# Four score tiles in five adjacent PSUM banks, and the FFN gate in SBUF

## The chip, the cores and the metric

The kernel runs on one core of one Trainium2 chip. The metric is the device time of one execution in microseconds (us); shown is the median of several runs. Beside it stands one execution taken by the hardware profiler, whose span goes from the first to the last instruction.

## The reference

Sparse attention is followed by a feed-forward network (FFN); all sizes are fixed.

```
q, k, v: 8 batches x 8 heads x 576 positions x 64      (float32)
scores = q @ k.T / 8;  keep scores >= max(row) - tau;  attn = softmax of those kept, sum + 1e-9
x = attn @ v, laid out as 4608 tokens x 512
h = x @ w_in (512 x 2048);  g = h if h >= 1, 0 if h <= -1, else (h + 1)^2 / 4
out = g @ w_out (2048 x 512)                            (float32; the weights arrive as float64)
```

## The kernel before

Each factor of a product is split into two float16 parts, high and low, and the product is made of three passes (high x high, high x low, low x high).

**Attention.** The 576 query rows of a head are cut into tiles of 128 rows; a tile's scores are 128 x 576 float32 in PSUM. A *visit* on TensorE (PE) computes two tiles at once, one of each head of a pair: the head dimension of 64 fills half of PE's rows, so the matmuls of the two heads run side by side. Each tile uses two PSUM banks, 288 columns in each (`s_ps`, two buffers); both buffers are taken by every visit. The rows that are left over are visited as a *tail*, 64 rows of two heads in one tile. The tile then goes through this chain (`add_tile`):

- DVE scales it in place and takes its minimum (L1039), and adds the threshold (L1043);
- ACT takes the exponential into SBUF, tile `e` (L1046);
- DVE masks it and sums the row (L1060), and takes the reciprocal (L1070);
- then one of three ways. Way "P", 283 of the 288 tiles: POOL scales `e` (L1078), ACT makes the high part `hl` (L1083), POOL the low part (L1086). Way "S", 3 tiles: DVE masks in PSUM (L1094), ACT makes the high part from there (L1102), DVE the low part (L1105). Way "T", 2 tiles: the transpose is done on PE;
- SP starts a DMA that transposes `hl` into `eT` (L1108), and PE multiplies by the values (L1184); ACT and DVE split that into `x` (L1192, L1196).

**FFN.** For 256 tokens at a time (128 in places), step by step of 256 or 512 hidden units: PE makes `ph` in PSUM (first product, L461), ACT takes relu and square into `asq` in SBUF (L1259, L1262), DVE forms the gate in place in `ph` (L1266), ACT makes the high part from `ph` (L1271, two instructions a step), DVE the low part from `ph` and the high part (L1276, two a step), both into `ga` and `gb` (some of whose buffers are free parts of the weight tiles `WI` and `WO`), and PE adds the second product into `acc` (L461). The PSUM ring `ph` has three banks; they also serve the attention-value product and small sums. PSUM is full: four banks for scores, three for `ph`, one for `acc`.

**Other work of two SBUF inputs on DVE.** The low part of some q and k tiles (L605, where `QHOW` has "D") and of the values (L661) is made by DVE from two tiles in SBUF.

**Order.** Every operation is an entry of a plan, with a cost and its buffers. The table `ORDER` gives the sequence in which a planner walks the entries; it computes a start for each from the costs, and the instructions are emitted in order of these starts, so each engine's queue is fixed by the program. SP's queue holds all DMA issues; an instruction in it that waits holds up those behind it. Small matmuls on `ones` (L1337) fill idle stretches of PE in the first 200 us.

Of the kernel before, what the change touches and what calls it, by code (L numbers as in the profile page):

```python
# [12 lines left out]
U32 = mybir.dt.uint32  # L13
AF = mybir.ActivationFunctionType
# [1379 lines left out]
```

## Time and profile before

| | us |
|---|---|
| median of 3 runs (1110.39 to 1111.41) | 1110.39 |
| the profiled execution | 1114.32 |
| its span | 1112.5 |
| PE busy in the span | 1080.0 (97%) |
| DVE busy | 898.6 (81%) |
| ACT busy | 871.3 (78%) |
| POOL busy | 789.5 (71%) |

Times in the rows are in us unless marked ns. Rows of groups give line, engine, operation, output and inputs, shape and count, then busy time, mean ns of one, and the idle time in front of them with what ended it. Rows of a timeline give start, duration and instruction. PEld is the loading of weights into PE, SPq the queue of SP. TensorE was granted 0.991 of its clock over the span.

### The profile page before, as it was taken

The numbers are of one execution on the slowest core, as the hardware profiler recorded it, in microseconds if no ns is written. First come the engines' busy times: TensorE is split into PE (matmuls) and PEld (weight loads), VectorE is DVE, ScalarE is ACT, GpSimd is POOL, SyncE is SP. The second block draws the span as 40 slices with busy tenths as digits, with TensorE's granted clock in tenths as the row PEclk, the third lists the DMA queues.
The fourth block names the chain that finished last, engine by engine and source line by source line (L and its number), as shares of the span: only waits on it lengthen the run. The fifth ranks groups of instructions, "written<-read, shape, count | busy, mean of one in ns | idle before, by whom it ended". The sixth has DMA issues, their size and how long they took to land.

```text
span 1112.5 us, 37005 instructions
## 1 busy us (share of the span) xinstructions
PE 1080.0 (97%) x14703; PEld 793.3 (71%) x14703; DVE 898.6 (81%) x2668; ACT 871.3 (78%) x1675; POOL 789.5 (71%) x921
## 2 busy tenths in 40 slices
PE   8689999999999999999999999999999999999998
PEld 7457657777777667776777677677777677777774
DVE  5899989998888887898788888788788898887222
ACT  6889769798797887887787888778788886776433
POOL 5889998786877987797768886666667987565000
PEclk9889999999999999999999999999999999999999
DMA  9887888688796997679867866759776686656000
GB/s 343 331 215 125 142 169 160 119 154 145 116 165 127 167 157 142 118 143 174 141 119 137 156 127 131 136 106 177 128 144 104 128 126 113 123 104 119 11 21 20
DMA packets 418046, 155.25 MB, mean 140 GB/s; under 512 B 396880, under 2 KB 396880, under 8 KB 417872
## 3 DMA queue, kind: packets, MB, share of 16 engines
q1 hardware_dynamic: 417872, 152.88, 70.9%
q8 instruction: 115, 1.88, 0.7%
q14 instruction: 59, 0.48, 0.1%
HBM read 45.09 MB, written 9.44 MB: 49 GB/s over the span
## 4 chain that ended last, share of the span: by engine, by line
PE 77%; DVE 8%; ACT 4%; DMA 4%; POOL 3%; issue 2%; SPq 0%; DVEq 0%; ACTq 0%; POOLq 0%
PE ph L461 30%; PE acc L461 28%; PE s L986 9%; PE ph L1184 8%; DMA eT<-hl 3%; DVE s L1039 2%; DVE e L1060 1%; POOL hl L1086 1%; ACT hl L1083 1%; PE ph L1337 1%; ACT e L1046 1%; POOL e L1078 1%; DMA raw<-in_k_dram 0%; DMA WO<-in_moe_w_in_dram 0%; DVE sm L1043 0%
## 5 line engine op out<-in xcount | busy, mean ns | idle before, releaser
L1086 POOL TENSOR_TENSOR hl<-e,hl 128x576 f16<-128x576 f32 x283 | 363.7, 1291 | 119.2 <-ACT hl L1083 112.4
L461 PEld LDWEIGHTS <-WI 128*64 128x64 f16 (+1 forms) x7458 | 408.0, 108 | 52.1 <-issue 15.1
L461 PE MATMUL ph<-x,WI 128*64 128x256 f16 (+1 forms) x6912 | 400.5, 264 | 0.3 <-DVE WI L1276 0.2
L1078 POOL TENSOR_SCALAR e<-e,sm 128x576 f32<-128x576 f32 x283 | 218.7, 776 | 77.8 <-DVE sm L1070 60.3
L1039 DVE TENSOR_SCALAR_CACHE_REDUCE s<-s,pc 128x576 f32<-128x576 f32 x288 | 230.9, 819 | 53.1 <-PE s L986 52.1
L1060 DVE SCALAR_TENSOR_TENSOR e<-s,sm,e 128x578 f32<-128x578 f32 x283 | 228.5, 814 | 29.3 <-ACT e L1046 21.5
L1046 ACT ACTIVATE e<-s,sm 128x576 f32<-128x576 f32 x288 | 209.7, 740 | 48.4 <-DVE s L1039 41.1
L1083 ACT ACTIVATE hl<-e 128x576 f16<-128x576 f32 x283 | 190.9, 681 | 55.5 <-POOL e L1078 38.8
L461 PE MATMUL acc<-WO,ga 128*64 128x512 f16 (+1 forms) x1596 | 203.3, 380 | 0.0
L1259 ACT ACTIVATE asq<-ph,fcs 128x512 f32<-128x512 f32 (+1 forms) x160 | 115.9, 735 | 44.7 <-PE ph L461 43.1
L1266 DVE SCALAR_TENSOR_TENSOR ph<-ph,fcs,asq 128x512 f32<-128x512 f32 (+1 forms) x160 | 111.3, 699 | 48.5 <-ACT asq L1262 47.7
L461 PEld LDWEIGHTS <-ga 128*64 128x64 f16 (+1 forms) x1596 | 92.5, 109 | 80.7 <-issue 9.0
L986 PE MATMUL s<-kk,qq 64*128 64x288 f16 (+1 forms) x1920 | 142.4, 286 | 7.3 <-DVE e L1060 4.3
L1184 PE MATMUL ph<-eT,vst 128*64 128x320 f16 (+2 forms) x1928 | 122.5, 279 | 7.1 <-DMA eT<-hl 3.8
L986 PEld LDWEIGHTS <-qq 64*128 64x128 f16 (+1 forms) x1920 | 80.9, 97 | 64.1 <-issue 45.7
L1184 PEld LDWEIGHTS <-vst 128*64 128x64 f16 x1928 | 100.6, 110 | 27.0 <-issue 12.4
L1262 ACT ACTIVATE asq<-asq 128x512 f32<-128x512 f32 x144 | 90.6, 630 | 3.1
L1276 DVE SCALAR_TENSOR_TENSOR ga<-ph,fcs,ga 128x256 f16<-128x256 f32 (+1 forms) x160 | 70.6, 449 | 23.8 <-ACT WO L1271 9.3
L1271 ACT ACTIVATE ga<-ph,fcs 128x256 f16<-128x256 f32 (+1 forms) x160 | 70.3, 450 | 24.0 <-DVE ph L1266 21.8
L461 PE MATMUL acc<-WO,gb 128*64 128x512 f16 (+1 forms) x576 | 73.9, 380 | 0.0
L461 PE MATMUL acc<-WO,WI 128*64 128x512 f16 (+1 forms) x546 | 69.9, 380 | 0.0
L461 PE MATMUL acc<-WO 128*64 128x512 f16 (+1 forms) x510 | 64.5, 380 | 0.0
(184 smaller groups left out, 1122.3 us busy)
## 6 DMA issues: line engine op xcount, KB each, us to landing
raw<-in_v_dram SPq DMA_DIRECT2D x32, 288.0 KB, 3.3
raw<-in_q_dram SPq DMA_DIRECT2D x32, 288.0 KB, 3.5
raw<-in_k_dram SPq DMA_DIRECT2D x32, 288.0 KB, 3.5
WO<-in_moe_w_in_dram SPq DMA_DIRECT2D x16, 512.0 KB, 7.7
out_dram<-ob SPq DMA_DIRECT2D x32, 256.0 KB, 2.5
x<-in_moe_w_out_dram SPq DMA_DIRECT2D x10, 512.0 KB, 5.6
eT<-hl SPq DMA_TRANSPOSE x286, 3.5
WO<-in_moe_w_out_dram SPq DMA_DIRECT2D x4, 512.0 KB, 5.0
```

What stands on the lines that cost most here:

```text
L461: T.matmul(out[x], lhsT[:, x], rhs, **flags)
L986: T.matmul(ap(sb, s_ps)[r, f, :SH], ap(qb, qq)[h, ql, c : c + r.stop - r.start], ap(kb, kk)[h, kl, f * SH : (f + 1) * SH], start=ql == kl ...
L1039: V.tensor_scalar(sv(), sv(), c[:, 24 + v : 25 + v], None, ALU.mult, ALU.min, accum_out=t[:, 0:1])
L1046: A.activation(ev(), sv(), AF.Exp, bias=ap(m, sm)[:, 0:1], scale=-1.0)
L1060: V.scalar_tensor_tensor(ev(SH + 1), sv(SH + 1), t[:, 2:3], ev(SH + 1), ALU.is_le, ALU.mult, accum_out=t[:, 3:4])
L1078: G.tensor_scalar(ev(), ev(), ap(m, sm)[:, 5:6], ESC, ALU.mult, ALU.mult)
L1083: A.activation(part2(0), ev(), AF.Copy)
L1086: G.tensor_tensor(part2(w), ev(), part2(0), ALU.subtract)
L1184: T.matmul(o[hd * D : (hd + 1) * D, :n], vt[:, k, hd * D : (hd + 1) * D], t[:, kb, (hd ^ p % 2) * n : ((hd ^ p % 2) + 1) * n], start=m == ...
L1259: A.activation(tv()[:, :, c], hv()[:, :, c], AF.Relu, bias=fcs[:, b, 2, q : q + 1], scale=fcs[:, b, 3, q : q + 1])
L1262: A.activation(ap(tb, asq), ap(tb, asq), AF.Square)
L1266: V.scalar_tensor_tensor(hv()[:, :, c], hv()[:, :, c], fcs[:, b, 0, q : q + 1], tv()[:, :, c], ALU.max, ALU.min)
```

## The change

From the second half of batch 1 on, a visit scores four tiles: two of each head, in one PSUM tile `s_all` of five adjacent banks. The tiles lie 578 columns apart and cross bank borders, so each is written in two pieces; the pieces of the two heads that run side by side lie in different banks. One bank holds pieces of both heads, the last of the first pair of tiles and one of the second pair; a no-op on SP (called the gate below, L1025 of the new kernel), which waits for PE's last write of the first and is waited for by PE ahead of the second, keeps these apart. Tails use the same tile. Of the 144 visits, 52 pairs of full ones become 52 visits of four; the fifth bank is taken from the ring `ph`, which keeps two.

In the FFN the gate is written into `asq` in SBUF instead of back into `ph` (L1377), and the high and low parts are made from there (L1382, L1387); the ring `asq` grows from two to four buffers. Way "S" is replaced by a way "V", taken by 32 tiles: DVE masks as in "P" and takes one more small operation, ACT makes the high part from `e` in SBUF, DVE the low part from `e` and `hl` (L1205). 255 tiles stay on "P" and one on "T". In the weights' preparation and for q and k some units change engines (`CONV`, `SIGN`, `QHOW`), and `ORDER` is a new table.

```diff
-CONV = {"i": "GGMGPGGPPPGPMPQP", "o": "PAPADPPAPDPDDADD"}
+CONV = {"i": "GGPGPGGPPPGPMPPQ", "o": "PAMADPPADGPPDAMD"}
-QHOW = "DDPDPPDPPPDPPPPPPPPPPPPPPDDPPPPP"
+QHOW = "DDPDPPDPPPDDPDPPPPPPPPPPPDDPPPPP"
+FOURS = 16
 ORDER = [
-    0, 54, 58, 59, 56, 57, 60, 623, 633, 638, 1, 4, 628, 5, 2, 55, 658, 61, 648, 653, 625, 643, 62, 63, 64, 900, 80, 624, 626, 627, 634, 75, 635, 636,
...
-TILE = {0: "T", 1: "T", 71: "S", 214: "S", 287: "S"}
+TILE = {0: "T", 1: "V", 3: "V", 21: "V", 25: "V", 33: "V", 38: "V", 53: "V", 74: "V", 78: "V",
...
-    s_ps = [pp.tile([P, 2, 512], F32, name=f"s{i}") for i in range(2)]
+    s_all = pp.tile([P, 5 * 512], F32, name="s")
+    s_ps = [s_all[:, i : i + 1024].rearrange("p (f n) -> p f n", f=2) for i in (0, 1024)]
-    ph = [pp.tile([P, 512], F32, name=f"ph{i}") for i in range(3)]
+    ph = [pp.tile([P, 512], F32, name=f"ph{i}") for i in range(2)] + [s_all[:, 2048:]]
-    asq = ring("asq", 2, [FW], F32)
+    asq = ring("asq", 4, [FW], F32)
...
+    def where(k):
+        x = sixth + k * (S + 2)
+        return x, -(-x // 512) * 512 - x
+    def add_four(js, slots):
+        toks = [plan.buf("s"), plan.buf("s")]
...
+            for a, z in ((0, 2),) if tail else ((0, 2), (1, 3)):
+                (fa, ca), (fz, cz) = pieces(at[a], a), pieces(at[z], z)
+                early, late = ((fz, 0, cz), (fa, 0, ca)), ((fz, cz, S), (fa, ca, S))
+                lows = ((0, 0), (0, 1), (1, 0))
+                walk = [(l, early + late) for l in lows] if not a else [(l, early) for l in lows] + [(l, late) for l in lows]
+                for (ql, kl), parts_ in walk:
+                    for fs, u, w in parts_:
+                        for f in fs:
+                            n = f(ql, kl, u, w)
+                        if fs is fz and not a and not u and ql and not tail:
+                            gate = Y.nop()
+                            tc.add_manual_dep(gate.ins, n.ins.name, DependencyInfo(DependencyClass.Sync, DependencyReason.DATA), reason="two row groups in a bank")
+                        if fs is fa and a and u and ql == kl == 0:
+                            tc.add_manual_dep(n.ins, gate.ins.name, DependencyInfo(DependencyClass.Sync, DependencyReason.DATA), reason="two row groups in a bank")
...
+        if not tail:
+            plan.op("SP", 0.75, lambda: None, behind=o)
...
+        def lo_v():
+            V.scalar_tensor_tensor(part2(w), ev(), ap(m, sm)[:, 5:6], part2(0), ALU.mult, ALU.subtract)
...
             def gate(hv=hv, tv=tv, g=g, q=q):
-                    V.scalar_tensor_tensor(hv()[:, :, c], hv()[:, :, c], fcs[:, b, 0, q : q + 1], tv()[:, :, c], ALU.max, ALU.min)
+                    V.scalar_tensor_tensor(tv()[:, :, c], hv()[:, :, c], fcs[:, b, 0, q : q + 1], tv()[:, :, c], ALU.max, ALU.min)
-                        A.activation(gv(h, 0)[:, :, c], hv()[:, 2 * h : 2 * h + 2, c], AF.Copy, scale=fcs[:, b, 1, q : q + 1])
+                        A.activation(gv(h, 0)[:, :, c], tv()[:, 2 * h : 2 * h + 2, c], AF.Copy, scale=fcs[:, b, 1, q : q + 1])
-                        V.scalar_tensor_tensor(gv(h, 1)[:, :, c], hv()[:, 2 * h : 2 * h + 2, c], fcs[:, b, 1, q : q + 1], gv(h, 0)[:, :, c], ALU.mult, ALU.subtract)
+                        V.scalar_tensor_tensor(gv(h, 1)[:, :, c], tv()[:, 2 * h : 2 * h + 2, c], fcs[:, b, 1, q : q + 1], gv(h, 0)[:, :, c], ALU.mult, ALU.subtract)
```

Three places in the order of the instructions follow. On PE, a visit before, in a batch's middle: `s` are the scores, `kk` and `qq` the split keys and queries; two tiles, 12 matmuls of 288 columns, then the attention-value product.

```order
L461 MATMUL acc<-WO,ga_107 64x512
L986 LDWEIGHTS qq_83
L986 MATMUL s_62<-kk_79,qq_83 128x288
L986 MATMUL s_61<-kk_79,qq_83 128x288
L1184 LDWEIGHTS vst_85
L1184 MATMUL ph_63<-eT_97,vst_85 64x320
```

And a visit now: 24 matmuls, the first pair of tiles in pieces of 252 and 384, 324 and 192 columns, the second of 186 and 318, 390 and 258.

```order
L1292 MATMUL ph_62<-eT_95,vst_83 64x320
L1006 LDWEIGHTS qq_78
L1006 MATMUL s<-kk_74,qq_78 128x252
L1006 MATMUL s<-kk_74,qq_78 128x384
L1006 MATMUL s<-kk_74,qq_78 128x324
L1006 MATMUL s<-kk_74,qq_78 128x192
L1006 MATMUL s<-kk_74,qq_78 128x186
L1006 MATMUL s<-kk_74,qq_78 128x318
L1006 MATMUL s<-kk_74,qq_78 128x390
L1006 MATMUL s<-kk_74,qq_78 128x258
L463 MATMUL acc<-WO,gb_112 64x512
```

The same columns are computed in 76 full visits where there were 128.

On DVE, before, between two visits: tile work on `s` and `e`, and an FFN step whose low parts read `ph` (PSUM) and `ga` or `WO` (SBUF).

```order
L1060 SCALAR_TENSOR_TENSOR e_92,sm_125<-s_62,sm_125,e_92 128x578
L1266 SCALAR_TENSOR_TENSOR ph_64<-ph_64,fcs,asq_98 128x512
L661 SCALAR_TENSOR_TENSOR vb_84<-raw_69,scs,vb_84 128x576
L1070 RECIPROCAL sm_125<-sm_125 128x1
L1276 SCALAR_TENSOR_TENSOR ga_108<-ph_64,fcs,ga_108 128x256
L1276 SCALAR_TENSOR_TENSOR WO<-ph_64,fcs,WO 128x256
L1039 TENSOR_SCALAR s_61,sm_122<-s_61,pc_116 128x2x288
```

And now, at such a place, with a tile of way "V":

```order
L1149 SCALAR_TENSOR_TENSOR e_88,sm_125<-s,sm_125,e_88 128x577
L1198 TENSOR_SCALAR sm_125<-sm_125 128x1
L1199 RECIPROCAL sm_125<-sm_125 128x1
L1377 SCALAR_TENSOR_TENSOR asq_96<-ph_63,fcs,asq_96 128x512
L1119 TENSOR_SCALAR s,sm_120<-s,pc_116 128x576
L1205 SCALAR_TENSOR_TENSOR hl_91<-e_88,sm_125,hl_91 128x576
L1387 SCALAR_TENSOR_TENSOR ga_108<-asq_96,fcs,ga_108 128x256
L1387 SCALAR_TENSOR_TENSOR WO<-asq_96,fcs,WO 128x256
```

The low parts of the FFN (L1387) and of the tile (L1205) now have both tensors in SBUF; before, this held for L605 and L661 (and the few L864 of the weights) alone.

On SP, before, with what each waits for (`hl` to `eT` are the transposes; a row shows the waits of the no-ops ahead of it too):

```order
L1108 DMA_TRANSPOSE eT_97<-hl_95 128x9x128 [waits DMAHW4_49,Activation_49,Pool_49]
L1328 DMA out_dram<-ob_100 64x512 [waits DMAHW5_49]
L1108 DMA_TRANSPOSE eT_97<-hl_94 128x9x128 [waits DMAHW6_49,Activation_49]
L629 DMA raw_70<-in_v_dram 128x576 [waits DMAHW7_49,Pool_49]
L1108 DMA_TRANSPOSE eT_97<-hl_93 128x9x128 [waits DMAHW0_49]
```

And now:

```order
L566 DMA raw_72<-in_k_dram 128x576 [waits DMAHW5_49,DVE_49]
L670 DMA_TRANSPOSE vst_84<-vb_82 128x14x128 [waits DMAHW6_49,PE_49]
L1208 DMA_TRANSPOSE eT_95<-hl_91 128x9x128 [waits DMAHW7_49,Pool_49]
L635 DMA raw_73<-in_v_dram 128x576 [waits PE_49,DMAHW0_49,Pool_49]
L1439 DMA out_dram<-ob_100 64x512 [waits DMAHW1_49]
```

The wait for PE in the fourth row is a gate's. It stands behind a transpose that waits for POOL, and PE's second half of the visit waits for it; 52 such gates were added to the queue.

More of the change, by code (lines that the diff above doesn't have):

```diff
@@ L514, in attn_ffn_kernel, with visit @@
     tiles, visits, ends = [], [], []
-    def visit(*both):
-        visits.append((len(tiles), len(tiles) + 1))
-        tiles.extend(both)
+    def visit(*some, at=None):
+        visits.append((range(len(tiles), len(tiles) + len(some)), at))
+        tiles.extend(some)
     for i, (b, p, q0, n) in enumerate(parts):
@@ L523, in attn_ffn_kernel @@
         y = 1 - x
-        for c in range(0, n - r, P):
-            visit((i, x, [(x, q0 + c)], c), (i, y, [(y, q0 + r + c)], n + r + c))
+        full = [((i, x, [(x, q0 + c)], c), (i, y, [(y, q0 + r + c)], n + r + c)) for c in range(0, n - r, P)]
+        if i >= FOURS:
+            visit(*full[0], *full[1], at=(1, 3, 0, 2))
+        else:
+            for f in full:
+                visit(*f)
         if not r:
@@ L684, in turn @@
             def turn(rb=rb, view=view, tb=tb):
-                padded["s"].discard(tb.slot)
+                padded["s"] -= {("old", tb.slot)} | {("new", k) for k in range(4)}
                 for k in range(nk):
@@ L968, in attn_ffn_kernel, with pieces, one, scores @@
     begun, prev = {}, {}
+    wide_s, sixth = [], 128
+    def where(k):
[3 more added lines that the diff above has]
+        toks = [plan.buf("s"), plan.buf("s")]
+        first = not wide_s
+        if first:
+            wide_s.append(plan.buf("ph"))
+        qks = {}
+        for j in js:
+            key = parts[tiles[j][0]][:2]
+            qks[key] = QK[key]
+        ready = [o for q in qks.values() for o in q[3]]
+        held = [b for q in qks.values() for b in q[1:3]]
+        tail = len(js) == 2
+        def pieces(j, k):
+            i, v, heads, col = tiles[j]
+            cb, qb, kb = QK[parts[i][:2]][:3]
+            x, cut = where(k)
+            made = []
+            for y, (hd, c) in enumerate(heads):
+                r = slice(0, P) if len(heads) == 1 else slice(y * D, (y + 1) * D)
+                h = slice(hd * D, (hd + 1) * D)
+                def one(ql, kl, a, z, r=r, h=h, c=c):
+                    return T.matmul(s_all[r, x + a : x + z], ap(qb, qq)[h, ql, c : c + r.stop - r.start], ap(kb, kk)[h, kl, a:z],
+                             start=ql == kl == 0, stop=ql == 1)
+                made.append(one)
+            return made, cut
+        def scores():
+            padded["s"] -= {("old", 0), ("old", 1)}
+            at = dict(zip(slots, js))
+            for a, z in ((0, 2),) if tail else ((0, 2), (1, 3)):
[12 more added lines that the diff above has]
+                            tc.add_manual_dep(n.ins, gate.ins.name, DependencyInfo(DependencyClass.Sync, DependencyReason.DATA), reason="two row groups in a bank")
+        o = plan.op("PE", 0.78 if tail else 1.48, scores, ready, take=toks + (wide_s if first else []), uses=held + wide_s, mode=3 if tail else 2)
+        if not tail:
+            plan.op("SP", 0.75, lambda: None, behind=o)
+        toks = toks + wide_s
+        lead, masks = [], []
+        for n, (j, k) in enumerate(zip(js, slots)):
+            masks.append(add_tile(j, toks, o, k, lead, masks[-1:] if n == len(js) - 1 else []))
+            if n == 1 and not tail:
+                lead = masks[:]
+            if j in ends:
+                add_av(ends[j])
@@ L977, in products @@
         def products(which):
+            padded["s"] -= {("new", k) for k in range(4)}
             for ql, kl in ((0, 0), (0, 1), (1, 0)):
@@ L1024, in sv @@
         def sv(w=SH):
-            return ap(s, s_ps)[:, :, :w]
-        ways = "PST" if not b else "PS"
+            if old:
+                return ap(s, s_ps)[:, :, :w]
+            x, _ = where(k)
+            return s_all[:, x : x + S + w - SH]
+        ways = "PSVT" if not b else "PSV" if old else "PV"
         flat = TILE.get(j, "P") == "T"
@@ L1045, in sexp @@
         def sexp():
+            padded["e"].discard((e.slot, not old))
             A.activation(ev(), sv(), AF.Exp, bias=ap(m, sm)[:, 0:1], scale=-1.0)
         def pads():
-            if e.slot not in padded["e"]:
-                padded["e"].add(e.slot)
-                V.memset(ap(e, es)[:, : 2 * (SH + 1)].rearrange("p (f n) -> p f n", f=2)[:, :, SH:], EPS / 2)
-            if s.slot not in padded["s"]:
-                padded["s"].add(s.slot)
-                V.memset(ap(s, s_ps)[:, :, SH : SH + 1], -3.0e38)
+            if (e.slot, old) not in padded["e"]:
+                padded["e"].add((e.slot, old))
+                if old:
+                    V.memset(ap(e, es)[:, : 2 * (SH + 1)].rearrange("p (f n) -> p f n", f=2)[:, :, SH:], EPS / 2)
+                else:
+                    V.memset(ap(e, es)[:, S : S + 1], EPS)
+            key = ("old", s.slot) if old else ("new", k)
+            if key not in padded["s"]:
+                padded["s"].add(key)
+                if old:
+                    V.memset(ap(s, s_ps)[:, :, SH : SH + 1], -3.0e38)
+                else:
+                    x, _ = where(k)
+                    V.memset(s_all[:, x + S : x + S + 1], -3.0e38)
         def smask():
@@ L1211, in add_av @@
                 xdone[g, x].append(o)
-    for at, both in enumerate(visits):
-        add_visit(at, both)
+    for at, (js, slots) in enumerate(visits):
+        if slots:
+            add_four(js, slots)
+        else:
+            add_visit(at, js)
     def wide(g):
@@ L1286, in attn_ffn_kernel @@
             o = plan.op("DVE", 0.665 + 0.263 * (m - 1), gate, [o], uses=[tb, hb])
-            o = plan.op("ACT", 0.718 + 0.285 * (m - 1), ghi, [o], take=[qs[0]], uses=[hb, qs[1]])
-            o = plan.op("DVE", 0.788 + 0.248 * (m - 1), glo, [o], uses=[hb, *qs])
+            o = plan.op("ACT", 0.718 + 0.285 * (m - 1), ghi, [o], take=[qs[0]], uses=[tb, qs[1]])
+            o = plan.op("DVE", 0.788 + 0.248 * (m - 1), glo, [o], uses=[tb, *qs])
             steps.append((fc, qs, gv, [o] + wo))
@@ L1330, in attn_ffn_kernel, with banks @@
                 plan.op("SP", 0.55, store, [o], uses=[ob], work=(0.68 * r / P, 0.65 * r / P, 1.6))
-    banks = [("ph", x, t[:, :P]) for x, t in enumerate(ph)] + [("acc", 0, accs[0][:, :P])] + [("s", x, t[:, 1, :P]) for x, t in enumerate(s_ps)]
+    def banks():
+        return [("ph", x, t[:, :P]) for x, t in enumerate(ph)] + [("acc", 0, accs[0][:, :P])] + [("s", x, t[:, 1, :P]) for x, t in enumerate(s_ps)]
     def keep_warm(bank, us):
@@ L1347, in gaps @@
                 until = {}
-                for p, x, bank in banks:
+                for p, x, bank in banks():
                     until[p, x] = min([t0 for q, y, t0, t1 in plan.held if (q, y) == (p, x) and t1 > free] + [o.t])
@@ L1351, in gaps @@
                 if end - free > 0.2:
-                    found += [(free, bank, min(gap, end - free)) for q, y, bank in banks if (q, y) == (p, x)]
+                    found += [(free, bank, min(gap, end - free)) for q, y, bank in banks() if (q, y) == (p, x)]
             free = max(free, o.t + o.cost)
@@ L1358, in attn_ffn_kernel @@
         plan.layouts(order)
+        if wide_s:
+            x = wide_s[0].slot
+            ph[x], ph[2] = ph[2], ph[x]
         left = gaps(order)
```

64 lines of the change are left out of this document (42 added, 22 removed), and 406 rows, old and new, of the table ORDER.

## The prediction

> **What bounds the kernel now.** I read the page's shares first, then the busy times by stretch.
>
> ```profile
> PE 1080.0 (97%) x14703; PEld 793.3 (71%) x14703; DVE 898.6 (81%) x2668; ACT 871.3 (78%) x1675; POOL 789.5 (71%) x921
> PE 77%; DVE 8%; ACT 4%; DMA 4%; POOL 3%; issue 2%; SPq 0%; DVEq 0%; ACTq 0%; POOLq 0%
> ```
>
> The second row is the chain that ended last, by engine: PE carries 77% of it. By stretch:
>
> ```profile
> 60.00:200.00 140.00, 133.22 (x1771) 96.83 (x1770) 130.30 (x393) 118.64 (x226) 129.50 (x148) 0.98 0.84 162
> 200.00:600.00 400.00, 396.95 (x5609) 293.66 (x5603) 345.98 (x1036) 333.18 (x643) 311.00 (x346) 1.00 0.78 141
> 600.00:1000.00 400.00, 398.10 (x5598) 292.64 (x5595) 335.25 (x990) 318.46 (x603) 289.82 (x317) 1.00 0.72 130
> 1000.00:1112.00 112.00, 107.80 (x1302) 75.94 (x1298) 44.61 (x117) 53.66 (x109) 15.31 (x16) 0.99 0.23 45
> ```
>
> The columns are PE, PEld, DVE, ACT, POOL, each busy us. From 200 to 1000 PE has 5 us of idle in 800, at full clock: it is the bound. But DVE is close behind, 345.98 + 335.25 = 681 us (85%), and POOL has 601 (75%). From 60 to 200 DVE and POOL are both at 93%. So two questions decide: what the change takes from PE, and what it puts on DVE.
>
> **What a visit costs PE.** Six rows of PE's timeline, start and duration first:
>
> ```profile
> 604.96 1.46 PE L461 MATMUL acc<-WO,gb 128*128 128x512 f16 x6
> 606.35 0.91 PE L986 MATMUL s<-kk,qq 64*128 64x288 f16 x12
> 607.19 1.49 PE L461 MATMUL acc<-WO,WI 128*64 128x512 f16 x12
> ...
> 608.60 2.79 PE L461 MATMUL ph<-x,WI 128*64 128x256 f16 x48
> 611.22 1.46 PE L461 MATMUL acc<-WO,WI 128*64 128x512 f16 x12
> 612.52 1.46 PE L461 MATMUL acc<-WO 128*64 128x512 f16 x12
> ```
>
> Durations overlap, so I use starts. From 611.22 to 612.52, 12 x 512 columns in two halves side by side, 3072 columns, take 1.30 us: 0.423 ns a column. The visit has 12 x 288 / 2 = 1728 columns, 0.73 us, but the next work starts after 0.84: 0.11 for turning away from it. The step ahead of it has 3072 columns and takes 1.39: 0.09 for turning towards it. A visit costs 0.20 us beyond its columns. The change drops 52 visits. Inside a visit of four the pieces are uneven: PE issues in order, so the longer piece of each two sets the pace; for the second pair (186 beside 318, then 390 beside 258) I count 1806 columns instead of 1728, 0.03 us lost. PE's gain is 52 x 0.17 = 8.8 us, all of it on the path while PE is the bound. Bounds: 0.25 a visit gives 13; nothing, if the piece borders cost as much as a turn, gives 0. I take 8.8, the value of the rows.
>
> **What moves to DVE, and what it meets there.** The FFN's low part keeps its shape, but its first input moves from PSUM (`ph`) to SBUF (`asq`), so both tensors lie in SBUF. The rows, grouped, all of one operation with the same kind of inputs:
>
> ```profile
> L661 DVE SCALAR_TENSOR_TENSOR vb<-raw,scs,vb 128x576 f16<-128x576 f32 x28 | 30.9, 1103 | 3.3 <-POOL vb L656 3.1
> L605 DVE SCALAR_TENSOR_TENSOR qq<-raw,pc,qq 128x576 f16<-128x576 f32 x7 | 6.9, 993 | 0.0
> L605 DVE SCALAR_TENSOR_TENSOR kk<-raw,pc,kk 128x576 f16<-128x576 f32 x7 | 6.3, 903 | 0.0
> L1105 DVE SCALAR_TENSOR_TENSOR hl<-s,sm,hl 128x576 f16<-128x576 f32 x3 | 2.4, 810 | 1.0 <-ACT hl L1102 1.0
> L1276 DVE SCALAR_TENSOR_TENSOR ga<-ph,fcs,ga 128x256 f16<-128x256 f32 x128 | 60.9, 476 | 21.0 <-ACT WI L1271 8.7 <-ACT WO L1271 8.1 <-ACT gb L1271 4.0
> L1078 POOL TENSOR_SCALAR e<-e,sm 128x576 f32<-128x576 f32 x283 | 218.7, 776 | 77.8 <-DVE sm L1070 60.3 <-DVE ph L469 9.1 <-DVE sm L1043 3.6
> L1086 POOL TENSOR_TENSOR hl<-e,hl 128x576 f16<-128x576 f32 x283 | 363.7, 1291 | 119.2 <-ACT hl L1083 112.4 <-issue 4.9 <-DMA eT<-hl 0.5
> L1043 DVE TENSOR_SCALAR sm<-sm,tcs 128x1 f32<-128x1 f32 x288 | 57.2, 208 | 4.5
> ```
>
> With `s` in PSUM 576 elements take 810 ns (L1105); with both tensors in SBUF the mean is 1103, 993 and 903. Why is seen in one place, DVE and POOL together:
>
> ```profile
> 132.61 1.77 DVE L661 SCALAR_TENSOR_TENSOR vb<-raw,scs,vb 128x576 f16<-128x576 f32 x1
> 132.50 1.27 POOL L1086 TENSOR_TENSOR hl<-e,hl 128x576 f16<-128x576 f32 x1
> 133.75 1.25 POOL L1078 TENSOR_SCALAR e<-e,sm 128x576 f32<-128x576 f32 x1
> ```
>
> POOL's low part began 0.11 us earlier and ended at 133.77. DVE's ended at 134.38, 0.61 later: it did its 576 elements only once POOL was through. POOL's next took 1.25 where its mean is 0.776: it waited for DVE in turn. So the two engines lock each other out where DVE has two SBUF inputs. The excess over 810 is 0.293 us (28 times), 0.183 (7) and 0.093 (7): 10.1 us in 42, 0.24 a piece.
>
> The Trainium skill (SBUF — State Buffer, Who interferes with whom) says that a DVE instruction with two SBUF inputs contends with a GpSimd instruction that reads SBUF, and that one with at most one SBUF input does not; POOL is GpSimd there. This trace agrees with the first half by the rows above; that the FFN's low part joins them no run here shows yet. If the page's rule holds for 256 elements as for 576, the next sum stands; if not, the first rival's does.
>
> How many: of the 320 low parts these lie where POOL is at work:
>
> ```profile
> 200.00:1000.00 800.00, 100.11 (x250) 1.00 0.75 135
> ```
>
> 250 x 0.24 = 60 us more on DVE from 200 to 1000. Bounds by the nearest rows: 0.093 and 0.293 a piece, 23 and 73; below nothing there is no way, a lock gives nothing back. I take 0.24, since the wait depends on what POOL is doing (776 to 1291 ns an instruction), not on DVE's size.
>
> Way "V": 25 of its 32 tiles come after 200 us. Each adds a low part (0.81 + 0.24) and one small operation (0.20, near L1043) to DVE, 1.25; the three "S" tiles go, -2.4: +29 us. POOL loses 25 x (0.776 + 1.291) = 52 us. `QHOW` moves q and k of two more pairs, in batches 2 and 3, to L605: four pieces of near 0.95, +4.
>
> DVE's need from 200 to 1000 becomes 681 + 60 + 29 + 4 = 774 us. How full DVE can be is read where it is fullest, 70 to 130:
>
> ```profile
> sum 60.00, PE 56.85 PEld 44.22 DVE 58.02 ACT 54.98 POOL 57.55; mean PE 18.95 PEld 14.74 DVE 19.34 ACT 18.33 POOL 19.18
> ```
>
> 58.02 of 60, 96.7%. 774 / 0.967 = 800 us without a single wait. PE would want 800 - 8.8 = 791. DVE's waits in this stretch:
>
> ```profile
> DVE s L1039 <- PE s L986: 47.3, 63, 2.7
> DVE e L1060 <- ACT e L1046: 17.4, 31, 2.7
> ```
>
> The first is DVE waiting for a visit. No visit can begin before all masks of the last (both before and now the scores have one set of buffers), so each leaves a hole of a visit's length unless FFN work fills it; half the visits leave half the holes, at most 24 us. A DVE that is behind finds exponentials ready, so the second goes. Between 0 and 24 I take 12. So 800 + 12 = 812, and DVE sets the pace.
>
> **The gate on SP.** PE waits in mid visit for a no-op that stands in SP's queue behind transposes:
>
> ```profile
> SPq L1108 <- POOL e L1078: 232.2, 111, 6.7
> SPq L1108 <- POOL hl L1086: 166.5, 68, 5.8
> 614.56 7.20 SPq L1108 DMA_TRANSPOSE eT<-hl  x3
> ```
>
> SP spends some 400 us waiting for POOL at the head of its queue; three transposes here took 7.2 us. What waits behind PE is the rest of the visit, all four tiles of DVE, and the FFN. Bounds a gate: 0 (SP free; between the write it waits for and the matmul that needs it PE has 324 + 954 columns, 0.54 us) and 2.4, a transpose's 7.2 / 3. In the new order most gates have over 2 us of PE work between them and the SP instruction ahead, so I take 0.1: 5 us, on DVE's path too since DVE waits for the visit. 817, so +17 from 200 to 1000.
>
> **The rest.** From 60 to 200: 7 tiles of "V" (8.8) and 26 low parts (6.2) come on DVE, and the weights give 2 back: 130.3 + 13 = 143 us, at 96.7% 148 of 140, up to +8; the new order could win back PE's idle 7. DVE and POOL are both at 93% and POOL loses 14, so between -7 and +8 I take +2, nearer to DVE's end. After 1000 PE has FFN alone and POOL 15 us: 0. ACT's high part reads SBUF; the square from SBUF takes 630 ns where relu from PSUM takes 778:
>
> ```profile
> L1259 ACT ACTIVATE asq<-ph,fcs 128x512 f32<-128x512 f32 x128 | 99.6, 778 | 36.2 <-PE ph L461 36.0
> L1262 ACT ACTIVATE asq<-asq 128x512 f32<-128x512 f32 x144 | 90.6, 630 | 3.1
> ```
>
> up to 37 us less on ACT, worth nothing, as ACT (81%) is not what others lack. The ring of two `ph` banks: a bank is held for the first product (2.6), relu, square and gate (2.2) instead of high and low part too; a step brings 2.6 + 2 x 1.3 us of PE work, so two banks cover it at 0 unless the gate on DVE is over 2 us late; then PE waits, inside the sum above. Splitting at bank borders changes no instruction count on DVE.
>
> Sum: +17 + 2 = +19 us on the profiled span of 1112.5, which lies 1.8 below its own execution's 1114.32; that is 3.9 above the median, and I put the difference on the median: 1110.4 + 19 = 1129.
>
> **Rivals.** (A) The lock is absorbed: DVE's wait rows are larger than what I keep, PE stays full, and only its gain counts: -8.8, or -4 with the gates' 5: 1102 to 1107. For it: 119 us of DVE idle in the 800. Against: 96.7% is DVE's best 60 us, and PE's pace needs DVE's extra work under 765 - 681 = 84 us (791 x 0.967 = 765); I have 93 without waits. It decides at (84 - 33) / 250 = 0.20 us a low part. (B) The gate is the wait that matters: PE stays the bound, but SP is late by 0.4 us a visit, a sixth of a transpose's 2.4. 52 x 0.4 = 21: 1102 + 21 = 1123. For it: the SP rows; against: the distances in the order. (C) Gain and losses cancel: within 2.2 us of 1110.4, if a low part costs near 0.2 and the waits are few.
>
> **How the numbers follow.** 0.2% (2.2 us) is about what a measurement of this kernel can tell from no change. DVE sets the pace: 0.52, 1129. B: 0.12. A: 0.27, 1102. C: 0.09. So faster 0.27, same 0.09, slower 0.64. Range: the top has 0.293 a piece (+13) and the waits half way to 24 (+6): 1148; the bottom is A's number with a little of the startup, 1100. About one in ten is left out at each end; the likeliest case alone has 1116 to 1148.
>
> **What the profile after would show.** Right: L1387 at 0.65 to 0.75 us instead of 0.476, in two clusters; DVE at 94% or more from 200 to 1000; PE with tens of us of idle ended by DVE; POOL's rows longer than 0.776 and 1.291. A visit of four taking 1.6 us with its turns and PE's waits for SP at L1006 under 10 us. Wrong: L1387 at 0.48, or PE still 99% busy; then A. PE idle ended by SP: B.

## The result, and the profile after

| | us | ratio to before, 95% interval |
|---|---|---|
| before, median on the same chip | 1110.9 | |
| after, median | 1330.9 | 1.199 [1.193, 1.204] |
| forecast | 1129 (1100 to 1148) | 1.017 |

The change is slower, as forecast, but by 220 us instead of 19, far outside the range.

The page's busy row of the kernel after, and then its stretches (columns as before):

```profile
PE 1136.4 (85%) x14739; PEld 861.2 (64%) x14739; DVE 1027.2 (77%) x2730; ACT 891.3 (67%) x1675; POOL 755.3 (57%) x863
```

```profile
60.00:200.00 140.00, 97.65 (x1027) 66.46 (x1026) 88.20 (x262) 80.78 (x149) 80.31 (x96) 0.82 0.52 113
200.00:1000.00 800.00, 693.54 (x9368) 527.79 (x9368) 677.90 (x1780) 566.71 (x1067) 491.07 (x532) 0.97 0.64 120
```

No engine is full. From 60 to 200 all of them lost about a third: DVE went from 130.30 to 88.20 us, POOL from 129.50 to 80.31, PE from 133.22 to 97.65. From 200 to 1000 PE has 693.54 instead of 795 and DVE 85% instead of the 94% forecast. When nobody is full, everybody waits for somebody. These rows tell who waited for whom in the two kernels, before first:

```profile
ACT e L1046 <- DVE s L1039: 41.1, 62, 2.3
DVE e L1060 <- ACT e L1046: 21.5, 39, 2.7
```

```profile
ACT e L1127 <- DVE s L1119: 101.9, 69, 5.7
DVE e L1149 <- ACT e L1127: 91.6, 112, 4.1
PE s L1006 <- DVE e L1149: 44.4, 34, 3.1
PE s L1006 <- SPq L1025: 11.7, 10, 2.4
PEld L1006 <- SPq L1025: 15.2, 11, 2.8
```

The columns are who waited, for whom, us in total, times, longest. The exponential (ACT) waits for DVE's row minimum 101.9 us instead of 41.1, the mask (DVE) for the exponential 91.6 instead of 21.5. The gate's two rows are small beside them. The timeline of the startup shows what kind of waits these are:

```profile
101.79 1.03 PE L1292 MATMUL s<-eT,vst 128*64 128x128 f16 x30 [0.31 <-DVE e L1149]
102.75 0.91 PE L1059 MATMUL s<-kk,qq 64*128 64x288 f16 x6
103.70 0.28 ACT L1300 ACTIVATE x<-s 128x128 f16<-128x128 f32 x1 [1.03 <-PE s L1059]
103.87 0.74 ACT L1127 ACTIVATE e<-s,sm 128x576 f32<-128x576 f32 x1
104.64 0.29 DVE L1304 SCALAR_TENSOR_TENSOR x<-s,x 128x128 f16<-128x128 f32 x1 [1.76 <-ACT e L1127]
```

The attention-value product lands in the FFN ring's third bank, which is now the last of the five of `s`; it is complete at 102.82. ACT's copy of it (L1300) starts at 103.70, when a score product into other banks has ended (102.75 + 0.91 = 103.66). DVE's half of it (L1304) starts at 104.64, when an exponential of other banks has ended (103.87 + 0.74 = 104.61). Neither has anything to do with what it waited for: they share only the name `s`.

How late each score product starts, against the same product of the kernel before (read from the two traces, us; products are counted from 0, and up to 335, the startup, both kernels visit two tiles):

```
score product no.     96    192    336    720   1200   1919
after                +49    +77    +98   +136   +170   +215
```

98 us are lost before the first visit of four.

### The profile page after: what moved, and what is told of

It reads as the page before. It is cut to its first block, busy times and chain, and to the rows that moved or that the text cites. A ratio compares the mean times of both kernels' runs of the same rounds, so it can differ in the third digit from the quotient of the medians.

```text
span 1335.8 us, 37182 instructions
## 1 busy us (share of the span) xinstructions
PE 1136.4 (85%) x14739; PEld 861.2 (64%) x14739; DVE 1027.2 (77%) x2730; ACT 891.3 (67%) x1675; POOL 755.3 (57%) x863
## 5 line engine op out<-in xcount | busy, mean ns | idle before, releaser
L463 PEld LDWEIGHTS <-WI 128*64 128x64 f16 (+1 forms) x7428 | 423.0, 110 | 73.6 <-issue 38.6
L1175 POOL TENSOR_TENSOR hl<-e,hl 128x576 f16<-128x576 f32 x255 | 333.7, 1314 | 200.0 <-ACT hl L1172 191.7
L463 PE MATMUL ph<-x,WI 128*64 128x256 f16 (+1 forms) x6480 | 382.2, 268 | 15.9 <-DVE asq L1377 7.7
L1127 ACT ACTIVATE e<-s,sm 128x576 f32<-128x576 f32 x288 | 203.8, 736 | 207.6 <-DVE s L1119 101.9
L1149 DVE SCALAR_TENSOR_TENSOR e<-s,sm,e 128x577 f32<-128x577 f32 (+1 forms) x287 | 231.9, 815 | 107.7 <-ACT e L1127 91.6
L1172 ACT ACTIVATE hl<-e 128x576 f16<-128x576 f32 x255 | 170.8, 676 | 61.4 <-POOL e L1167 58.2
L1006 PE MATMUL s<-kk,qq 64*128 64x318 f16 (+11 forms) x1584 | 104.1, 289 | 56.5 <-DVE e L1149 44.4
L1377 DVE SCALAR_TENSOR_TENSOR asq<-ph,fcs,asq 128x512 f32<-128x512 f32 (+1 forms) x149 | 101.9, 694 | 20.2 <-ACT asq L1373 19.2
L1387 DVE SCALAR_TENSOR_TENSOR ga<-asq,fcs,ga 128x256 f16<-128x256 f32 (+1 forms) x160 | 106.0, 669 | 14.6 <-ACT ga L1382 14.0
L1382 ACT ACTIVATE ga<-asq,fcs 128x256 f16<-128x256 f32 (+1 forms) x160 | 75.8, 481 | 42.8 <-DVE asq L1377 37.5
L1059 PE MATMUL s<-kk,qq 64*128 64x288 f16 (+1 forms) x336 | 39.0, 325 | 35.0 <-DVE e L1149 15.9
```

The source lines that it names most:

```text
L463: T.matmul(out[x], lhsT[:, x], rhs, **flags)
L1006: return T.matmul(s_all[r, x + a : x + z], ap(qb, qq)[h, ql, c : c + r.stop - r.start], ap(kb, kk)[h, kl, a:z], start=ql == kl == 0, stop= ...
L1127: A.activation(ev(), sv(), AF.Exp, bias=ap(m, sm)[:, 0:1], scale=-1.0)
L1149: V.scalar_tensor_tensor(ev(SH + 1), sv(SH + 1), t[:, 2:3], ev(SH + 1), ALU.is_le, ALU.mult, accum_out=t[:, 3:4])
L1172: A.activation(part2(0), ev(), AF.Copy)
L1175: G.tensor_tensor(part2(w), ev(), part2(0), ALU.subtract)
```

## The experiments

Theory 1: the five banks are one tile of the program, which makes an access to a part of a tile wait for the last access to any other part; the waits above are between accesses that share no bank. Theory 2: the lock of DVE and POOL on two SBUF operands, by way of DVE's time. Theory 3: the gate on SP. Theory 4: the order table and the ring of two banks.

**One tile in the kernel before.** Two kernels, one with all five banks in one tile and one with the four score banks alone; the edit of the first:

```diff
-    s_ps = [pp.tile([P, 2, 512], F32, name=f"s{i}") for i in range(2)]
+    s_all = pp.tile([P, 5 * 512], F32, name="s")
+    s_ps = [s_all[:, i : i + 1024].rearrange("p (f n) -> p f n", f=2) for i in (0, 1024)]
-    ph = [pp.tile([P, 512], F32, name=f"ph{i}") for i in range(3)]
+    ph = [pp.tile([P, 512], F32, name=f"ph{i}") for i in range(2)] + [s_all[:, 2048:]]
```

> The kernel before, with one edit: the two score buffers and the third bank of the FFN ring become views of one five-bank PSUM tile. Instructions, operands' addresses, order table and visits of two tiles stay. Theory 1 (waits between disjoint parts of one tile: the program makes an access to one part of the tile wait for the last access to any other part): the startup, whose visits are of two tiles in both kernels, lost 98 us in the kernel after by the 336th score matmul, so this kernel loses about as much there and more behind it: 1200 to 1400 us, with the rows 'exp waits for DVE's row minimum' and 'mask waits for exp' grown as in the kernel after. Theory 2 (the lock of DVE and POOL on two SBUF inputs), theory 3 (the gate on SP's queue) and theory 4 (the order table and the FFN ring of two banks): none of the three is in this kernel, so 1109 to 1113 us.

Measured: 1529.0 us, 1.376 [1.374, 1.378], above the 1200 to 1400 expected. At product 336 it is 96.5 us late, the kernel after 97.7: the startup's loss is reproduced by allocation alone. From 200 to 1000 PE is left with 77% and DVE with 63%:

```profile
200.00:1000.00 800.00, 619.75 (x7875) 445.85 (x7875) 507.40 (x1473) 475.85 (x906) 453.88 (x505) 0.93 0.55 103
```

> The kernel before, with only the two score buffers as views of one four-bank tile; the three FFN banks stay tiles of their own. Theory 1: the score tiles still wait for each other, the attention-value product and the FFN no longer wait for scores; between a third and all of the loss of the kernel with the five-bank tile, 1150 to 1400 us. Theories 2, 3 and 4: 1109 to 1113 us.

Measured: 1188.2 us, 1.069 [1.067, 1.071]. 77 of the 417 us come from the two score buffers waiting for each other; the other 340 need the FFN's bank in the same tile, which ties scores, FFN, values and weights together. The share is below the third that was expected.

**The same tile, with waits by bank.** Every call on an engine goes through a wrapper (so that all its rows have one line, L434) that takes away the waits for other banks of `s` and names those for its own:

```diff
+            for y, ybanks, yrest in reversed(done[-600:]):
+                if banks & ybanks:
+                    if not found:
+                        found = True
+                        keep.append(y)
+                        tc.add_manual_dep(x, y.name, DependencyInfo(DependencyClass.Sync, DependencyReason.DATA), reason="the same bank")
+                elif rest & yrest:
+                    keep.append(y)
+            tc.declare_no_dep(x, group=other, keep=keep, reason="other banks of the tile")
```

> The kernel before with the five-bank tile (the edit that gave 1529 us), and now each access to that tile waits only for the last access of each other engine to a bank that it touches itself; a wait for an access to other banks is taken away. Theory 1 (the 417 us were waits between accesses to different banks of one tile): back to the time of before, 1109 to 1125 us. Against it (the addresses or something else about the one tile cost the time): 1400 to 1530 us.

Measured: 1117.7 us, 1.005 [1.004, 1.007]. 411 of 417 us are gone with the waits alone; addresses, banks and the engines' instructions are those of 1529 us. Theory 1 is shown. This kernel is 5.6 us above its own before (1112.1).

> The kernel after, with one thing changed: each access to the five-bank tile waits only for the last access of each other engine to a bank that it touches itself. Two neighbouring tiles of a visit of four still lie in a common bank and still wait for each other. Theory 1: the startup's 98 us come back and most of the 117 us behind it; what stays is the lock (50 us in the kernel before by itself) and the waits within common banks: 1130 to 1200 us. Theory 4 (the new order table and the FFN ring of two banks do not fit): at most the startup's part comes back, 1230 to 1330 us. Theory 3 (the gate): what stays above before is about the waits of PE for SP, some 27 us.

Measured: 1179.4 us, 1.061 [1.060, 1.063]. 152 of the 220 us were waits between different banks; at product 336 the delay is 10.6 us instead of 97.7. Theory 4 alone would have left 1230 or more. Waits stay by bank, not by column, as the Trainium skill (PSUM — Partial Sum Buffer, PSUM bank collisions raise a hardware error) asks for, by which two engines may not use one bank on the same 32 partitions at once, even at different columns; no run here shows such a collision.

What is left is what the prediction had drawn, DVE close to full; the stretch, and the page's busy row:

```profile
200.00:1000.00 800.00, 743.08 (x10384) 571.82 (x10382) 741.58 (x1940) 624.21 (x1177) 539.78 (x581) 0.99 0.69 128
```

```profile
PE 1089.7 (92%) x14739; PEld 827.7 (70%) x14739; DVE 1028.5 (87%) x2730; ACT 892.5 (76%) x1675; POOL 759.7 (64%) x863
```

PE is idle 57 us in this stretch. The two largest groups of that idle time end with DVE: with the gate of the FFN, which frees one of the two banks left in the ring `ph`, and with the mask, which frees the scores' banks for the next visit:

```profile
PE ph L434 <- DVE asq L434: 20.5, 21, 4.0
PE s L434 <- DVE e L434: 11.0, 15, 1.6
```

**The lock alone, in the kernel before**, and its removal from the kernel after. The edit of the first (with the ring `asq` of four); the second is its reverse, and since the order table gives the FFN's bank away after the gate, its high and low parts may be made from the product that comes next:

```diff
-                    V.scalar_tensor_tensor(hv()[:, :, c], hv()[:, :, c], fcs[:, b, 0, q : q + 1], tv()[:, :, c], ALU.max, ALU.min)
+                    V.scalar_tensor_tensor(tv()[:, :, c], hv()[:, :, c], fcs[:, b, 0, q : q + 1], tv()[:, :, c], ALU.max, ALU.min)
...
-                        V.scalar_tensor_tensor(gv(h, 1)[:, :, c], hv()[:, 2 * h : 2 * h + 2, c], fcs[:, b, 1, q : q + 1], gv(h, 0)[:, :, c], ALU.mult, ALU.subtract)
+                        V.scalar_tensor_tensor(gv(h, 1)[:, :, c], tv()[:, 2 * h : 2 * h + 2, c], fcs[:, b, 1, q : q + 1], gv(h, 0)[:, :, c], ALU.mult, ALU.subtract)
```

> The kernel before, with one edit: the FFN's gate goes into SBUF (a ring of four buffers), and the high and the low part are read from there; scores, visits, banks and order stay. Theory 2 (the lock): the row of the low part grows from 449 to about 670 ns, 35 us of DVE over 160 tiles, and the end goes with DVE: 1130 to 1150 us if the lock is what cost the kernel after its time in the four-tile phase, and at most that. Theory 1: the row grows the same way, but its cost is only what DVE lacks in slack, 0 to 15 us, 1108 to 1126 us. Theories 3 and 4: 1109 to 1113 us.

Measured: 1162.1 us, 1.046 [1.043, 1.048]: 50 us, more than either theory had. The groups of the low part, of this kernel and then of the kernel before (the largest of four each):

```profile
L1276 DVE SCALAR_TENSOR_TENSOR ga<-asq,fcs,ga 128x256 f16<-128x256 f32 (+1 forms) x160 | 111.7, 705 | 13.6 <-ACT ga L1271 13.0 <-ACT WO L1271 0.2
```

```profile
L1276 DVE SCALAR_TENSOR_TENSOR ga<-ph,fcs,ga 128x256 f16<-128x256 f32 (+1 forms) x160 | 70.6, 449 | 23.8 <-ACT WO L1271 9.3 <-ACT WI L1271 8.7 <-ACT gb L1271 5.6
```

Over all four groups 230.1 us instead of 141.0. Sorted by what the POOL instruction under way still had to run when the low part began (from the traces, mean us of one, the pieces of 256 elements alone):

```
POOL has left, us       none   to 0.2   to 0.5   to 0.9   to 1.5
ph and ga (before)      0.48    0.48     0.47     0.48     0.48
asq and ga (this one)   0.48    0.59     0.63     0.96     1.17
```

With one operand in PSUM POOL does not matter; with both in SBUF DVE waits until POOL is through: of the 115 pieces that began with 0.5 us or more of a POOL instruction left, 101 ended 0.26 to 0.29 us after that instruction. The other 14 took 0.47 to 0.48 us and ended 0.53 to 0.54 us before it. That is the rule of the Trainium skill (SBUF — State Buffer, Who interferes with whom) which the prediction named, now seen on the FFN's own instruction of 256 elements.

The price shows on PE, in its wait for DVE's mask ahead of a visit, over the whole span, before first:

```profile
PE s L986 <- DVE e L1060: 4.3, 9, 0.8
```

```profile
PE s L986 <- DVE e L1060: 35.0, 48, 1.9
```

> The kernel after, with one edit: the gate stays in the FFN's PSUM bank, as before. Theory 1: nothing that the chain waits for is touched, or the FFN's bank is held longer: 1310 to 1350 us. Theory 2: the lock was the cost, so most of the 220 us come back: 1110 to 1180 us. Theories 3 and 4: within 10 us of the kernel after, 1320 to 1340 us.

Measured: 1337.2 us, 1.205 [1.202, 1.207]. While the tile-wide waits rule, DVE's 78 us less (948.8) buy nothing.

**What DVE's time costs.** In the kernel before, one more operation in PSUM behind each half of the low part; no lock, nothing for POOL:

```diff
+                        V.tensor_scalar(hv()[:, 2 * h, c], hv()[:, 2 * h, c], 1.0, 0.0, ALU.mult, ALU.add)
```

> The kernel before, with one more DVE operation behind each half of the FFN's low part: 128 (or fewer) columns of the gate's PSUM bank multiplied by 1 in place, 320 operations of an estimated 0.2 to 0.28 us (between the profile's rows of 91 ns and more for one column and 340 ns for 128 to 256 columns out of PSUM), no second SBUF operand, nothing more for POOL. If 50 us for 89 us of longer rows is the price of DVE time (theory 2 in that form): 64 to 90 us more of DVE cost 37 to 52 us, 1148 to 1163 us. If the lock costs through POOL or otherwise, and DVE's 15% of slack hides its own work: 1111 to 1130 us.

Measured: 1174.0 us, 1.056 [1.054, 1.057]. That is above the 1148 to 1163 expected, as the operations took more than estimated; DVE has 1001.0 us instead of 898.6; the group, and the stretch:

```profile
L1277 DVE TENSOR_SCALAR ph<-ph 128x128 f32<-128x128 f32 (+1 forms) x320 | 91.6, 286 | 11.1
```

```profile
200.00:1000.00 800.00, 761.67 (x10529) 563.49 (x10525) 716.81 (x2155) 618.96 (x1187) 573.62 (x637) 1.00 0.69 129
```

61.7 / 102.4 = 0.60 us for each us of DVE; with the lock 50.4 / 85.7 (984.3 - 898.6) = 0.59. So the lock costs about what other DVE time costs, and it costs this although DVE stands at 90% here and PE at 95%: neither is full, and the kernel is 62 us slower. The added operation also holds the FFN's bank longer, so its price is not DVE's time alone. PE's waits, over the whole span:

```profile
PE s L986 <- DVE e L1060: 26.3, 42, 2.2
PE ph L461 <- DVE ph L1277: 10.8, 14, 1.3
```

**DVE's extra time, taken from the kernel with waits by bank.** First the low part as a product with a single SBUF operand (it comes out as zero):

```diff
-                        V.scalar_tensor_tensor(gv(h, 1)[:, :, c], tv()[:, 2 * h : 2 * h + 2, c], fcs[:, b, 1, q : q + 1], gv(h, 0)[:, :, c], ALU.mult, ALU.subtract)
+                        V.tensor_scalar(gv(h, 1)[:, :, c], tv()[:, 2 * h : 2 * h + 2, c], fcs[:, b, 1, q : q + 1], 0.0, ALU.mult, ALU.mult)
```

> The kernel after with the waits of its own banks alone (1179 us), and the FFN's low part is a product with one SBUF input: the high part is not subtracted, everything else is as it was. Theory 2 in its share (what is left above before is the lock): the row of the low part falls from 0.70-0.79 to 0.45 us or less, DVE has some 90 us less to do and falls from 93% to 85% of the stretch from 200 to 1000, and the time falls by about the 50 us that the same lock cost the kernel before: 1115 to 1140 us. If what is left is the common banks, the gate or the order table: the row falls as well, and the time stays within 15 us, 1164 to 1179 us.

Measured: 1150.7 us, 1.035 [1.033, 1.037], between the two. The row fell only half way, from 703 to 578 ns:

```profile
L434 DVE TENSOR_SCALAR ga<-asq,fcs 128x256 f16<-128x256 f32 (+1 forms) x160 | 91.1, 578 | 6.4 <-PE acc L434 5.9
```

By POOL's remaining time a piece of 256 elements takes 0.38 us with none left and 1.30 with 0.9 or more: this form waits for POOL too. So the run took 45 us from DVE (983.7), not 90, and 29 from the time.

Then POOL's two operations of a tile in halves (`for y in range(2)` around each, half the columns):

> The kernel after with the waits of its own banks alone (1179 us), and POOL's two operations of a tile are each issued as two of half the columns; all results stay. If the low part's row is long because DVE waits for the POOL instruction that is under way (the lock), halves cut that wait by some 60%: row of the low part from 0.74 to about 0.58 us, DVE 40 to 50 us less, 1135 to 1160 us, against some 80 us more work on POOL. If the row is long for another reason (two SBUF inputs are slow by themselves): the row stays and the time is 1175 to 1200 us.

Measured: 1178.8 us, 1.060 [1.057, 1.064]. The row did fall, so it waits for the POOL instruction under way, though less than expected, from 703 to 651 ns:

```profile
L434 DVE SCALAR_TENSOR_TENSOR ga<-asq,fcs,ga 128x256 f16<-128x256 f32 (+1 forms) x160 | 103.2, 651 | 16.0 <-ACT ga L434 15.4
L434 POOL TENSOR_TENSOR hl<-e,hl 128x288 f16<-128x288 f32 x510 | 377.8, 765 | 116.2 <-ACT hl L434 112.2 <-issue 2.0 <-DMA eT<-hl 0.8
L434 POOL TENSOR_SCALAR e<-e,sm 128x288 f32<-128x288 f32 x510 | 282.0, 566 | 70.6 <-DVE sm L434 57.9 <-ACT ga L434 2.5 <-DVE ph L434 2.3
```

POOL pays 110 us for the halves (759.7 to 869.5), ACT's wait for it grows from 54.8 to 97.6 us, and what DVE gains, 24 us (1004.8), is lost again.

Then DVE's work given to POOL, in the hope of a version that beats both: way V's low part by two POOL operations, and in two further runs the FFN's low part of some steps (every third step below, every second in the last run):

```diff
+            G.tensor_scalar(ev(), ev(), ap(m, sm)[:, 5:6], 1.0, ALU.mult, ALU.mult)
+            G.tensor_tensor(part2(w), ev(), part2(0), ALU.subtract)
...
+            if len(steps) % 3:
+                o = plan.op("DVE", 0.788 + 0.248 * (m - 1), glo, [o], uses=[tb, *qs])
+            else:
+                o = plan.op("POOL", 2.0, plo, [o], uses=[tb, *qs])
```

> The kernel after with the waits of its own banks alone (1179 us), and the low part of the 32 tiles of way V is made by two POOL operations in place of one of DVE. Theory 2 as DVE time: DVE 32 us less, POOL 65 to 70 us more, at 0.58 us for each us of DVE 18 us less: 1158 to 1168 us. If POOL's chain or the common banks are what is left: 1175 to 1195 us.

> The same, and beside it the FFN's low part of three steps in eight (two in four) made on POOL, by one product in place and two subtractions. DVE about 120 us less than at 1179 us, back near the 899 us of the kernel before; POOL some 180 us more, 940 us. Theory 2 as DVE time: 68 us come back, less what PE gains: 1100 to 1125 us. If POOL's longer queue becomes the wait: 1150 to 1200 us.

> The same with every second step on POOL: DVE some 145 us less than at 1179 us, POOL some 215 us more. Theory 2 as DVE time: 1098 to 1120 us. If POOL becomes the bound: slower than with three steps in eight, 1130 to 1200 us.

Measured: 1191.2, 1249.1 and 1253.5 us, all slower than 1179.4, and the last two above every range expected. In the second DVE is back at 930.7 us, and among its waits are:

```profile
ACT hl L434 <- POOL e L434: 137.4, 82, 5.9
POOL asq L434 <- ACT gb L434: 46.5, 6, 21.8
```

POOL stands up to 21.8 us in front of a low part whose high part ACT has not made yet, and all its tiles stand behind. The order table was kept, with POOL's new work put where DVE had done it; a table made for it was not tried.

Last, the low parts set to zero by a short operation, in the kernel with waits by bank and, as a control, in the kernel before:

```diff
-                        V.scalar_tensor_tensor(gv(h, 1)[:, :, c], tv()[:, 2 * h : 2 * h + 2, c], fcs[:, b, 1, q : q + 1], gv(h, 0)[:, :, c], ALU.mult, ALU.subtract)
+                        V.memset(gv(h, 1)[:, :, c], 0.0)
```

> The kernel after with the waits of its own banks alone (1179 us), and the FFN's low parts are set to zero by a short DVE operation in place of being computed (the remainders are left out). An estimate of 0.15 us for each makes DVE's sum 1028 - 236 + 48 = 840 us, less than the 899 us of the kernel before. If DVE's time is all that is left of the 68 us, the gain of the visits of four shows now: 1095 to 1112 us, and faster than the control by 0 to 9 us. If the common banks, the gate, the order table or the ring of two banks cost something of their own: 1115 to 1150 us, and slower than the control.

> The control: the kernel before, its low parts set to zero by the same short operation. DVE falls from 899 to about 806 us. If DVE's time costs 0.6 us for each us at its margin in this direction too, 1055 us; if TensorE is the bound of the kernel before, which has 1080 us of work in it, 1095 to 1111 us.

Measured: 1117.5 us, 1.005 [1.004, 1.007], and 1112.0 us, 1.001 [1.000, 1.002]. The control: DVE has 72 us less (826.3) and the time stays, so TensorE does bound the kernel before, and DVE's price of 0.6 goes upward only. The other: 62 of the remaining 68 us go with the low part's time on DVE, and 5.5 stay, where the visits of four should have gained. Order table, ring of two, gate and visits of four, their gains included, thus come to no more than these 5.5 while DVE has time to spare; whether a ring of three would have saved some of the 62 was not tried. Nor need the 5.5 come from them: one tile with waits by bank left 5.6 in the kernel before as well, and no run separates the two. From 200 to 1000, this kernel and then the control:

```profile
200.00:1000.00 800.00, 783.02 (x11132) 601.98 (x11130) 652.49 (x2064) 658.89 (x1239) 554.65 (x613) 1.00 0.74 135
```

```profile
200.00:1000.00 800.00, 797.35 (x11239) 587.53 (x11235) 625.62 (x2034) 652.87 (x1249) 603.75 (x665) 1.00 0.74 136
```

The gain itself is there in PE's work. The score products of the whole span, this kernel and then the control:

```profile
L434 PE MATMUL s<-kk,qq 64*128 64x288 f16 (+12 forms) x1920 | 134.4, 285 | 15.9 <-SPq L1075 7.5
```

```profile
L986 PE MATMUL s<-kk,qq 64*128 64x288 f16 (+1 forms) x1920 | 142.2, 286 | 7.1 <-DVE e L1060 4.7
```

They take 7.8 us less, but from 200 to 1000 PE is idle 17 us where the control has 2.7. The largest group of that idle time, in the same stretch:

```profile
PE s L434 <- SPq L1075: 7.5, 12, 2.0
```

**The gate.** Two runs added eight empty SP instructions behind each gate (`for _ in range(8): gate = Y.nop()`):

> The kernel after with the waits of its own banks alone (1179 us), and the gate of a visit of four made longer by eight more empty SP instructions. Theory 3 (PE's wait for the gate is on the path): the time grows by about 52 times what eight of them take, 0.3 to 0.5 us: 1195 to 1205 us. Theory 2 (DVE is the bound, PE has 15 us in 200 to spare): within 6 us, 1176 to 1186 us.

> The kernel after with the waits of its own banks alone and its low parts set to zero (1117 us), and eight more empty SP instructions behind each gate. In that kernel PE has 17 us of idle from 200 to 1000, and the largest group of it that the program explains is ended by SP's gate. Theory 3 in that place (where DVE is not the bound, PE's wait for the gate is on the path): the time grows by 52 times what the eight take, an estimate of 5 to 25 us: 1122 to 1142 us, and PE's wait for SP grows by as much. If the gate is hidden there too: 1114 to 1120 us.

Measured: 1178.3 and 1118.0 us. They say nothing of the gate: both traces have the same 469 semaphore instructions on SP as without the edit, so the gate did not become longer. The next edit does stay in the program; the gate now waits for a later product, the last of the first pair of tiles:

```diff
-                        if fs is fz and not a and not u and ql and not tail:
+                        if fs is fa and not a and u and ql and not tail:
```

> The kernel after with the waits of its own banks alone and its low parts set to zero (1117 us), and the gate waits for the last product of the first pair of tiles instead of the last one in the common bank: of the 0.54 us of PE work that covered the gate, 0.14 us are taken away (324 of 1278 columns). Theory 3 in that place (the gate is on PE's path): up to 52 x 0.14 = 7 us more, 1120 to 1125 us, and PE's and PEld's waits for SP (7.5 and 11.6 us from 200 to 1000) grow by 3 to 7 us. If SP is late because of the transposes ahead of the gate, and not because the gate is asked late: within 3 us, 1114 to 1120 us.

Measured: 1116.7 us, 1.005 [1.003, 1.006], and PE's wait for SP is 5.9 us instead of 7.5. How early the gate is asked for does not matter here; that SP comes late because of what stands ahead of it fits, but no run took that away. A kernel without the gate was not tried, since two row groups could then write one bank at the same time.

## Why the prediction was wrong, step by step

- **The failed step: "Splitting at bank borders changes no instruction count on DVE", and no other term for the new tile.** The diff's `s_all` and `ph = ... + [s_all[:, 2048:]]` were read as addresses. They are also what the program orders by: scores of two visits, the FFN's third bank, values and weights became one thing to wait for. Its size: 152 us of 220, 87 of them by product 336 (97.7 late with the tile-wide waits, 10.6 with waits by bank). For the startup the forecast had +2, all of it from the work on the engines. The direction was forecast right, but from the smaller part of the loss, the other 68 us.
- **"How full DVE can be": the term mis-sized.** The prediction let DVE fill up to 96.7% for nothing and charged only what was above. By that sum the lock alone would have been free: (681 + 60) / 0.967 = 766 of 800 us. It cost 50. The fullest 60 us, from 70 to 130, are no measure for the 800 from 200 on: with more on DVE, DVE and PE both stopped short (90% and 95%, 93% and 93%), and each us of DVE cost 0.6 on average over the first 86 and over the first 102. The prediction had DVE waiting for visits, at most 24 us; the rows show the reverse as well, PE waiting for DVE's masks (35.0 us with the lock alone, 4.3 before). With 130 us more on DVE (1028.5 - 898.6) that is 78 us, near the 68 measured. Why the price is 0.6 is not shown; fixed queues on both sides are an argument only.
- **The lock: right in kind, a little small.** 0.24 us a piece was taken for the stretch from 200 to 1000. With the lock alone the mean there went from 0.449 to 0.755 us, 0.31 more and just above the upper bound of 0.293 (89.1 / 320 = 0.28 over the whole span). In the kernel after 145 of the 256 pieces of 256 elements take 0.47 to 0.49 us and the others up to 1.59, not in one second cluster; POOL's rows grew to 829 and 1314 ns. Way V's low part took 1084 ns, 1.05 forecast.
- **Rival A (the lock is absorbed) is refuted** by 1162 us with the lock alone. Rival C falls with it.
- **PE's gain of 8.8 us: in PE's work, not in the time.** A visit of four takes 1.57 us to the start of the next work (613.94 to 615.51), as forecast, and the score products are 7.8 us shorter than the control's; yet at equal FFN work the kernel is 5.5 us behind the control, as PE is idle more. "All of it on the path" did not hold.

```profile
613.94 1.65 PE L1006 MATMUL s<-kk,qq 64*128 64x252 f16 x24
615.51 0.30 PE L463 MATMUL ph<-x,WI 128*64 128x256 f16 x2
```

- **The gate, rival B: small.** PE's and PEld's waits for SP, 11.7 and 15.2 us, are over the 10 given, but no part of the 152 or the 62. With the low parts at zero it ends 7.5 of the 17 us of PE's idle time; how much of the lost 8.8 is the gate's stays open.
- **The shown signs.** "DVE at 94% or more" was wrong for the kernel after (85%) and nearly right once the waits were by bank (93%): the forecast described that kernel, at 1179 us, and was 50 us short of it.

The shares belong to this order of removal: with the tile-wide waits in place, taking the lock away gave nothing. No version here beats the kernel before.

## What to carry to other kernels

When a change merges buffers, ask what the program orders by: one tile for five banks made unrelated engines wait for each other, at 152 us here and 417 us in the kernel before, and naming the waits by bank took nearly all of it back. Look for such waits in the timeline: an instruction that starts when one ends with whose data it has nothing to do. And price an engine's extra time by a dummy operation on it rather than by its free share: at a DVE of 85% each us still cost 0.6.

## What the runs showed of the hardware

- A DVE instruction with one SBUF operand waited for POOL as well, when it was a product from SBUF to SBUF: 256 elements took 0.38 us with POOL free and 1.30 with 0.9 us or more of a POOL instruction left. Setting zeros in the same buffers did not wait (0.165 us for each of the 256 pieces of full size). The Trainium skill (SBUF — State Buffer, Who interferes with whom) names `tensor_scalar` among the operations that can take both ports by themselves; the trace agrees. The section clears an instruction with one SBUF input only outside these modes of two ports, and the prediction left that condition out.
- From 60 to 200 TensorE was granted 0.82 of its clock in the kernel after, with PE busy 70%, and 0.98 in the kernel before, with 95%. How much of the 220 us that adds was not separated.
